# RWKV6 attention and a gated dense layer in one kernel: the boot in written order, level 16 copied by ScalarE, and h - tanh(h) of the first block summed by an accumulating transfer

## The chip, the cores and the metric

One core of a Trainium2 chip. TensorE multiplies matrices; VectorE and ScalarE work element by element; SyncE and GpSimd here mostly issue transfers, which the 16 DMA engines carry out. The metric is the device time of an execution in microseconds (us), taken as the median of several. Executions of one kernel here lie within about 1% of each other; all the runs told below are in the fast state, so they may be compared. The runs came in batches, a1 to a4 on another chip than b1, a5 to a7 and a10 to a13, so between batches the ratio to the kernel before is the safer measure. Profiles are of single executions of the same kernels; a profiled span is some 2 us shorter than the time of the same execution.

## The reference

```python
# attention: B, H, S, D = 4, 8, 768, 48; state is (B, H, D, D), starts at 0
for t in range(S):
    y[:, :, t] = einsum('bhd,bhde->bhe', r_t, state + (u * k_t) v_t^T)
    state = w_t[..., None] * state + k_t v_t^T
x = y.transpose(0, 2, 1, 3).reshape(3072, 384)
# dense part: w_in 384 x 2048, w_out 2048 x 384, both float64 in memory
h = x @ w_in
g = h - tanh(h)
out = g @ w_out
```

The recurrence is computed in chunks of 64 tokens, doubling a block size m: for m = 1, 2, 4, 8, 16 and 32 TensorE forms the products of one half of each block with the other ("level m"), VectorE multiplies by decays between levels, then come "turn" (transposes), "update" (states) and "result". In the program kq, rp, wt and v hold k, r, w and v of a block; kmix and rmix are k and r with every second token multiplied by u, for level 1. xT is the result as the dense part reads it; its last part lands in `late`, from which six small transfers fill the holes of xT.

## The kernel before

The 3072 tokens go through in 8 blocks of 384. The dense part of a block has 16 steps f of 128 columns of w_in. A step is three matmuls into `hp`, six ScalarE instructions, five VectorE instructions, and three steps later three matmuls into `acc`. The attention of block i+1 is woven into the steps of block i as phases. Block 0 has nobody ahead of it: its attention is the boot, and during boot and block 0 the float64 weights are converted as well, two ScalarE and three VectorE instructions for each f.

```python
def convert(f, raw, _):
    ...
    nc.scalar.activation(out=a.bitcast(F32), in_=hi.bitcast(F32), func=AF.Copy, scale=HIGH_SCALE)
    nc.scalar.activation(out=up, in_=lo.bitcast(U32), func=AF.Copy, scale=2.0 ** -29)
    return [
        lambda: nc.vector.tensor_single_scalar(a, a, 3, op=ALU.logical_shift_left),
        lambda: nc.vector.scalar_tensor_tensor(out=a, in0=hi, scalar=-2 ** 31, in1=a,
                                               op0=ALU.bitwise_and, op1=ALU.bitwise_or),
        lambda: nc.vector.tensor_tensor(out=a, in0=a, in1=up, op=ALU.add)]

def first(xT, f, ps):
    hp = ps.tile([P, NB], F32, name="hp", tag="hp")
    for kc in range(KC):
        nc.tensor.matmul(hp, lhsT=w_in_sb[:, f, kc, :], rhs=xT[:, kc, :], ...)
    ...
    nc.scalar.activation(out=h, in_=hp, func=AF.Copy, scale=1.0 / UPSCALE)
    nc.scalar.activation(out=s, in_=h, func=AF.Square)
    nc.scalar.activation(out=qa, in_=s, func=AF.Square, bias=shift[:, 0:1])
    nc.scalar.activation(out=qb, in_=s, func=AF.Square, bias=shift[:, 1:2])
    nc.scalar.activation(out=th, in_=h, func=AF.Tanh)
    nc.scalar.activation(out=big, in_=s, func=AF.Relu, bias=shift[:, 2:3])
    ...
    return g, [
        product(hs, h, SERIES, s, ALU.mult),
        lambda: nc.vector.tensor_tensor(out=th, in0=h, in1=th, op=ALU.subtract),
        product(hs, qa, QUAD[0][1], hs, ALU.add),      # a series for small h
        product(g, qb, QUAD[1][1], hs, ALU.add),
        lambda: nc.vector.copy_predicated(out=g, mask=big.bitcast(I32), data=th)]

# plan of block 0: at which f each phase of block 1 stands, and where weights are converted
names = ("level 1", 2, 4, 8, 16, 32, "turn", "update", "result")
steps = (1, 2, 3, 4, 5, 6, 8, 10, 12)
before = {0: ("kmix", "rmix", "totals 1", "totals 2", "kq")}   # kmix, rmix: times u, on VectorE
converted = (0, 3, 4, 5, 5, 8, 9, 10, 11, 11)

ctx.enter_context(tc.manual_schedule(engines={PE, SP}))   # boot: VectorE, ScalarE ordered by the scheduler
```

The VectorE instructions of step f are issued behind the ScalarE instructions of step f+1, with the conversions between them.

Of the kernel before, what the change touches and what calls it, by code (L numbers as in the profile page):

```python
# [83 lines left out]
def kernel(  # L84
# [24 lines left out]
    for i, value in enumerate((QUAD[0][0], QUAD[1][0], -SMALL)):  # L109
# [9 lines left out]
    mask_cols = {1: slice(0, 64), 2: slice(64, 96), 4: slice(96, 128), 8: slice(128, 160),  # L119
                 16: slice(160, 192)}  # L120
    mask_all = const.tile([P, 192], I8, name="mask_all", tag="mask_all")
# [60 lines left out]
    class Block:  # L182
# [27 lines left out]
        def mix(self, p0, n):  # L210
            rmix, kmix, rp, kq = (self.tiles[x] for x in ("rmix", "kmix", "rp", "kq"))

            def part(t, p, k, odd):
                return t[:, p * NB:(p + k) * NB].rearrange("d (n two) -> d n two", two=2)[:, :, odd]

            for t, src, odd in ((kmix, kq, 1), (rmix, rp, 0)):
                nc.vector.tensor_copy(out=part(t, p0, n, 1 - odd), in_=part(src, p0, n, 1 - odd))
                for p in range(p0, p0 + n):
                    nc.scalar.activation(out=part(t, p, 1, odd), in_=part(src, p, 1, odd),  # L219
                                         func=AF.Copy, scale=u_sb[:, p:p + 1])  # L220
# [21 lines left out]
        def level_1(self, ps, p0):  # L242
            gr = self.gram(ps, self.tiles["kmix"], self.tiles["rmix"], p0, UP, 1, L)
            mask = masks[1].bitcast(U8).rearrange("s b j -> s (b j)").unsqueeze(1).unsqueeze(1)
            nc.vector.copy_predicated(
                out=A[:, :, p0:p0 + UP].rearrange("s h p c t -> s h (p c) t"),
                mask=mask.to_broadcast([P, 2, UP * NCP, L]),
                data=gr.rearrange("s h (n t) -> s h n t", t=L))
# [24 lines left out]
        def level(self, ps, m, p0, n):  # L273
            if m == L // 2:
                self.last_level(ps, p0, n)
                return self.decay(m, p0, n)
            gr = self.gram(ps, self.tiles["kq"], self.tiles["rp"], p0, n, m, L // 2)
            ins = self.decay(m, p0, n)
            nb = L // (2 * m)
            for h in range(2):  # L280
                dst = A[:, h, p0:p0 + n].rearrange("s p c (b two m) -> s (p c) b two m",
                                                   two=2, m=m)[:, :, :, 1, :]
                src = gr[:, h].rearrange("s (n b m) -> s n b m", b=nb, m=m)
                mask = masks[m].bitcast(U8).unsqueeze(1).to_broadcast([P, n * NCP, nb, m])
                nc.vector.copy_predicated(out=dst, mask=mask, data=src)  # L285
            return ins
# [39 lines left out]
        def update(self, ps, p0):  # L326
# [17 lines left out]
            for c in range(NCH - 1 if last else NCH):  # L344
                for p in range(UP):
                    dst = St[:, p0 + p, c + 1, 0:D] if c + 1 < NCH else                         states[self.q + 1][:, p0 + p, 0, 0:D]
                    n0 = (p * NCP + c // 2) * D
                    k = (i0 + p) * NCH + c
                    nc.vector.scalar_tensor_tensor(  # L349
                        out=dst, in0=St[:, p0 + p, c, 0:D], scalar=tot[:, k:k + 1],  # L350
                        in1=kvp[:, c % 2, n0:n0 + D], op0=ALU.mult, op1=ALU.add)

# [57 lines left out]
        def phase(self, ps, name):  # L410
            if name == "level 1":
                for p0 in HALVES:
                    self.level_1(ps, p0)
# [36 lines left out]
        def start(self, ps, background):  # L450


            for p0 in HALVES:
                for name, src in (("kq", kT), ("rp", rT), ("wt", wT)):
                    self.load(name, src, p0, UP)
            for name in ("rmix", "kmix"):
                self.tiles[name] = inp.tile([P, NPAIR * NB], F32, name=name, tag=name)
            yield
            for p0 in HALVES:
                self.mix(p0, UP)  # L460
                self.level_1(ps, p0)
                self.decay(1, p0, UP)
                self.totals(1, p0, UP)
            for m in (2, 4, 8, 16, 32):
                for p0 in HALVES:
                    ins = self.level(ps, m, p0, UP)
                    self.totals(m, p0, UP)

                tc.add_manual_dep(background.pop(0)().ins, ins.ins.name, mybir.DependencyInfo(
                    mybir.DependencyClass.Sync, mybir.DependencyReason.DATA))  # L470
            for p0 in HALVES:
                self.turn(ps, p0)
            background.pop(0)()
            for p0 in HALVES:
                self.update(ps, p0)
            for p0 in HALVES:
                self.result(ps, list(range(p0, p0 + UP)), p0 != HALVES[0])
                if p0 == HALVES[0]:
                    self.fill_holes([nc.sync, nc.scalar, nc.sync, nc.scalar, nc.sync, nc.sync])
            yield  # L480


    def first(xT, f, ps):
# [13 lines left out]
        nc.scalar.activation(out=th, in_=h, func=AF.Tanh)  # L497
# [4 lines left out]
        def product(out, in0, scalar, in1, op0):  # L502
# [4 lines left out]
            product(hs, h, SERIES, s, ALU.mult),  # L507
            lambda: nc.vector.tensor_tensor(out=th, in0=h, in1=th, op=ALU.subtract),  # L508
# [24 lines left out]
    def plan(i):  # L533

        names = ("level 1", 2, 4, 8, 16, 32, "turn", "update", "result")
        if i == 0:

            steps = (1, 2, 3, 4, 5, 6, 8, 10, 12)
            before = {0: ("kmix", "rmix", "totals 1", "totals 2", "kq")}
            behind = {1: ["rp"]}  # L540
            converted = (0, 3, 4, 5, 5, 8, 9, 10, 11, 11)
# [9 lines left out]
    ctx.enter_context(tc.manual_schedule(engines={PE, SP}))  # L551
    with tc.tile_pool(name="ps_boot", bufs=4, space=PSUM) as boot:
        xT = blocks[0].begin()
        raws = []

        def more_weights():
            raws.append(load_weights(len(raws), nc.sync))
            return raws[-1][-1]

        def ahead(name, src):  # L560
            return lambda: blocks[1].load(name, src, 0, NPAIR)

        background = [ahead("rmix", rT), ahead("kmix", kT), ahead("wt", wT)]
        background += [more_weights for _ in range(3, RAWS)] + [ahead("kq", kT)]
        start = blocks[0].start(boot, background)
        next(start)
        more_weights()
        blocks[0].load_v()
        for f in (1, 2):
            more_weights()  # L570
        next(start)
        for f in range(AHEAD):
            for op in convert(*raws.pop(0)):
                op()
            raws.append(load_weights(f + RAWS, nc.gpsimd))
    ps_d = ctx.enter_context(tc.tile_pool(name="ps_d", bufs=1, space=PSUM))
    ps_a = ctx.enter_context(tc.tile_pool(name="ps_a", bufs=2, space=PSUM))
    with tc.manual_schedule(engines={DVE, ACT}):
        blocks[1].prepare("load 3")
        waiting, rest, extra = [], [], []  # L580
        loaded = AHEAD + RAWS
        for i, blk in enumerate(blocks):
            here = xT
            later = blocks[i + 1] if i + 1 < len(blocks) else None
            after = blocks[i + 2] if i + 2 < len(blocks) else None
            if later:
                xT = later.begin()
            phases, before, behind, converted = plan(i)
            second = Second(blk.b * S + blk.q * NB, ps_d)
            for f in range(NF):  # L590
                g, next_rest = first(here, f, ps_d)
                waiting.append((second, f, g))

                for n, op in enumerate(rest):
                    op()
                    if n >= 2 and extra:
                        extra.pop(0)()
                for op in extra:
                    op()
                rest = next_rest  # L600
                if later:
                    for name in before.get(f, ()):
                        later.prepare(name)
                    if f in phases:
                        later.phase(ps_a, phases[f])
                    for name in behind.get(f, ()):
                        block = after if name.startswith("load") else later
                        if block:
                            block.prepare(name)
                extra = []  # L610
                for _ in range(converted.count(f)):
                    extra += convert(*raws.pop(0))
                    if loaded < NF:
                        raws.append(load_weights(loaded, nc.gpsimd))
                        loaded += 1
                if len(waiting) > LAG:
                    s, fs, gs = waiting.pop(0)
                    s.add(fs, gs)
        for op in rest:
            op()  # L620
        for s, fs, gs in waiting:
            s.add(fs, gs)
# [47 lines left out]
```

## Time and profile before

The time is 679.96 us in the runs at hand before the prediction. What matters of its profile, with the rows themselves in the prediction below:

| event | us |
|---|---|
| state updates of the boot begin | 33.55 |
| first dense matmul (hp) | 49.47 |
| level-2 products of block 1 begin | 63.58 |
| level-32 products of block 1 begin, after a wait of 1.55 | 88.93 |
| last acc matmul of block 0 ends | 146.6 |
| profiled span | 678.6 |

The prediction reads it in three stretches: the boot, block 0, and the rest, in which TensorE is busy 99% of the time. So the table is a list of milestones: a gain is one only if the last acc of block 0 comes earlier, and nothing behind it is made longer.

### The profile page before, as it was taken

The page shows a single profiled execution, that of the slowest core. Times are in us where ns is not written, and L with a number is a line of the kernel's source. Part 1 is how long each engine was busy: PE and PEld are TensorE (multiplying, and loading weights), DVE is VectorE, ACT ScalarE, POOL GpSimd, SP SyncE. Part 2 cuts the span into 40 slices and gives each one's busy share as a digit, 9 for nine tenths or more (in the row PEclk, how much of TensorE's full clock was granted, in tenths as well). Part 3 has the DMA queues.
Part 4 walks back from the last instruction along what each step waited for, and adds up shares of the span by engine and source line. Part 5 has one row for each costly group of instructions (what it writes and reads, how often), then busy time and mean ns, then how long its engine had stood idle before and what let it go on. Part 6 is the DMA issues. An engine that isn't in the chain of part 4 may idle for free.

```text
span 678.6 us, 19964 instructions
## 1 busy us (share of the span) xinstructions
PE 643.7 (95%) x8480; PEld 412.9 (61%) x8480; DVE 567.3 (84%) x1139; ACT 470.2 (69%) x920; POOL 9.8 (1%) x30
## 2 busy tenths in 40 slices
PE   3847999999999999999999999999999999999997
PEld 3734656656665666656665666656666566655554
DVE  7899999999986998689984999769986899756764
ACT  4346779985677757686576856777576865768785
POOL 2010000000000000000000000000000000000000
PEclk9968989999999999999999999999999999999999
DMA  8788141204012321025012140124110200001000
GB/s 312 219 286 319 67 140 47 92 36 142 2 50 90 98 80 50 10 82 176 3 48 92 36 141 3 48 90 142 38 48 15 98 17 2 1 11 36 0 0 36
DMA packets 30840, 54.36 MB, mean 80 GB/s; under 512 B 2336, under 2 KB 28704, under 8 KB 30752
## 3 DMA queue, kind: packets, MB, share of 16 engines
q1 hardware_dynamic: 28960, 44.20, 19.6%
q0 software_dynamic: 1584, 8.65, 3.6%
q8 instruction: 67, 1.10, 0.7%
q10 hardware_dynamic: 208, 0.25, 0.1%
q14 instruction: 21, 0.17, 0.1%
HBM read 47.19 MB, written 4.72 MB: 76 GB/s over the span
## 4 chain that ended last, share of the span: by engine, by line
PE 78%; DVE 7%; issue 4%; PEld 4%; DMA 3%; ACT 3%; PEldq 0%; SPq 0%; DVEq 0%; ACTq 0%
PE acc L524 33%; PE hp L486 31%; PE att L238 9%; DVE states L349 2%; PE att L386 2%; PEld hp L486 2%; PE att L321 2%; PEld att L368 1%; DMA raw<-in_weights 1%; PE att L302 1%; DMA xT<-late 1%; PEld acc L524 1%; DMA wt<-in_wT 1%; DVE kq L270 1%; DVE hs L503 1%
## 5 line engine op out<-in xcount | busy, mean ns | idle before, releaser
L486 PE MATMUL hp<-xT,w_sb 128*128 128x384 f32 x768 | 273.4, 493 | 8.4 <-DMA xT<-late 6.8
L524 PE MATMUL acc<-w_sb,gT 128*128 128x384 f32 x768 | 275.0, 495 | 0.0
L486 PEld LDWEIGHTS hp<-xT,w_sb 128*128 128x128 f32 x768 | 147.6, 193 | 112.5 <-ACT up L169 7.0
L524 PEld LDWEIGHTS acc<-w_sb,gT 128*128 128x128 f32 x768 | 140.7, 190 | 89.2 <-ACT o L529 2.3
L493 ACT ACTIVATE h<-hp 128x384 f32<-128x384 f32 x128 | 62.7, 490 | 163.0 <-PE hp L486 162.4
L508 DVE TENSOR_TENSOR th<-h,th 128x384 f32<-128x384 f32 x128 | 70.9, 554 | 43.2 <-ACT th L497 43.1
L503 DVE SCALAR_TENSOR_TENSOR hs<-h,s 128x384 f32<-128x384 f32 x128 | 71.0, 555 | 23.2 <-ACT s L494 23.0
L511 DVE COPY_PREDICATED gT<-big,th 128x384 f32<-128x384 int32 x128 | 76.1, 595 | 12.8 <-ACT th L497 0.5
L495 ACT ACTIVATE qa<-s,shift 128x384 f32<-128x384 f32 x128 | 78.8, 615 | 4.2
L503 DVE SCALAR_TENSOR_TENSOR gT<-qb,hs 128x384 f32<-128x384 f32 x128 | 71.4, 558 | 9.7 <-PE hp L486 0.5
L498 ACT ACTIVATE big<-s,shift 128x384 f32<-128x384 f32 x128 | 76.8, 600 | 0.0
L496 ACT ACTIVATE qb<-s,shift 128x384 f32<-128x384 f32 x128 | 76.7, 599 | 0.0
L503 DVE SCALAR_TENSOR_TENSOR hs<-qa,hs 128x384 f32<-128x384 f32 x128 | 70.6, 551 | 0.0
L494 ACT ACTIVATE s<-h 128x384 f32<-128x384 f32 x128 | 67.0, 524 | 4.1
L238 PEld LDWEIGHTS att<-rp,kq 48*64 48x64 f32 x3072 | 54.7, 148 | 22.5 <-issue 18.9
L497 ACT ACTIVATE th<-h 128x384 f32<-128x384 f32 x128 | 64.9, 507 | 0.0
L238 PE MATMUL att<-rp,kq 48*64 48x32 f32 x3072 | 58.4, 231 | 6.1 <-issue 6.0
L270 DVE TENSOR_TENSOR kq<-kq,tot 128x768 f32<-128x768 f32 (+1 forms) x45 | 38.7, 859 | 2.6 <-PE att L238 2.6
L285 DVE COPY_PREDICATED scores<-mask_all,att 128x384 f32<-128x384 uint8 (+1 forms) x72 | 40.3, 621 | 0.0
L270 DVE TENSOR_TENSOR rp<-rp,tot 128x768 f32<-128x768 f32 (+1 forms) x45 | 38.8, 863 | 0.0
L349 DVE SCALAR_TENSOR_TENSOR states<-states,tot,att 128x48 f32<-128x48 f32 x176 | 31.5, 256 | 6.7 <-PE att L339 6.7
L238 PE MATMUL att<-rmix,kmix 48*64 48x64 f32 x768 | 14.5, 232 | 8.8 <-ACT rmix L219 6.1
(50 smaller groups left out, 338.8 us busy)
## 6 DMA issues: line engine op xcount, KB each, us to landing
raw<-in_weights POOLq DMA_DIRECT2D x11, 768.0 KB, 6.7
rmix<-in_rT SPq DMA_DIRECT2D x7, 768.0 KB, 4.7
kmix<-in_kT SPq DMA_DIRECT2D x7, 768.0 KB, 6.5
wt<-in_wT SPq DMA_DIRECT2D x7, 768.0 KB, 7.3
kq<-in_kT SPq DMA_DIRECT2D x7, 768.0 KB, 4.4
rp<-in_rT SPq DMA_DIRECT2D x7, 768.0 KB, 4.8
v_sb<-in_v SPq DMA_DIRECT2D x8, 576.0 KB, 5.7
out_y<-o SPq DMA_DIRECT2D x23, 192.0 KB, 2.0
```

What stands on the lines that cost most here:

```text
L238: nc.tensor.matmul(dst, lhsT=lhs[rows, t0:t0 + L], rhs=src, start=True, stop=True)
L270: ins = nc.vector.tensor_tensor(out=part, in0=part, in1=by, op=ALU.mult)
L486: nc.tensor.matmul(hp, lhsT=w_in_sb[:, f, kc, :], rhs=xT[:, kc, :], start=(kc == 0), stop=(kc == KC - 1))
L494: nc.scalar.activation(out=s, in_=h, func=AF.Square)
L495: nc.scalar.activation(out=qa, in_=s, func=AF.Square, bias=shift[:, 0:1])
L496: nc.scalar.activation(out=qb, in_=s, func=AF.Square, bias=shift[:, 1:2])
L497: nc.scalar.activation(out=th, in_=h, func=AF.Tanh)
L498: nc.scalar.activation(out=big, in_=s, func=AF.Relu, bias=shift[:, 2:3])
L503: return lambda: nc.vector.scalar_tensor_tensor(out=out, in0=in0, scalar=scalar, in1=in1, op0=op0, op1=ALU.mult)
L508: lambda: nc.vector.tensor_tensor(out=th, in0=h, in1=th, op=ALU.subtract),
L511: lambda: nc.vector.copy_predicated(out=g, mask=big.bitcast(I32), data=th)]
L524: nc.tensor.matmul(acc, lhsT=g[:, j * P:(j + 1) * P], rhs=w_out_sb[:, f, :], start=(f == 0), stop=(f == NF - 1))
```

## The change

The intent is to relieve VectorE where it is the fuller engine, and to start the dense part earlier. Five things are done at once: the boot is written out in order for VectorE and ScalarE, with two whole conversions ahead of the state updates; block 1's two multiplications by u go to ScalarE in the boot; level 16 needs no mask any more and is copied by ScalarE; in block 0 tanh(-h) is computed and a transfer of GpSimd adds h to it, in place of VectorE's subtraction; phases, conversions and weight loads are put at other places. Core of the diff:

```diff
-    ctx.enter_context(tc.manual_schedule(engines={PE, SP}))
+    ctx.enter_context(tc.manual_schedule(engines={PE, SP, DVE, ACT}))
@@ level: no mask for level 16
+            if 2 * m % 32 == 0:
+                for par in range(2):
+                    for b in range(nb):
+                        ...
+                        nc.scalar.copy(out=dst[:, :, :, t0:t0 + m], in_=src[:, :, :, b, :])
+                return ins
@@ first
-        nc.scalar.activation(out=th, in_=h, func=AF.Tanh)
+        nc.scalar.activation(out=th, in_=h, func=AF.Tanh, scale=-1.0 if by_dma else 1.0)
+        if by_dma:
+            nc.gpsimd.dma_start(out=th, in_=h, accum_op=ALU.add)
...
-            product(hs, h, SERIES, s, ALU.mult),
-            lambda: nc.vector.tensor_tensor(out=th, in0=h, in1=th, op=ALU.subtract),
+            product(hs, h, SERIES, s, ALU.mult)] + ([] if by_dma else [
+            lambda: nc.vector.tensor_tensor(out=th, in0=h, in1=th, op=ALU.subtract)]) + [
@@ plan of block 0
-            steps = (1, 2, 3, 4, 5, 6, 8, 10, 12)
-            before = {0: ("kmix", "rmix", "totals 1", "totals 2", "kq")}
+            steps = (1, 2, 3, 5, 7, 9, 10, 11, 13)
+            before = {0: ("totals 1", "totals 2", "kq")}
-            converted = (0, 3, 4, 5, 5, 8, 9, 10, 11, 11)
+            converted = (0, 3, 3, 4, 5, 6, 10, 10, 11, 12)
@@ boot (written out; cut to its end)
+            if m <= 8:
+                ready.append(convert(*raws.pop(0)))
+            if m in (8, 16):
+                later.mix(0, NPAIR, ("rmix" if m == 8 else "kmix",), copies=False)
+        converted()
+        for p0 in HALVES:
+            blk.turn(ps, p0)
+        converted()
+        for _ in range(2):
+            ready.append(convert(*raws.pop(0)))
+        begin_behind(blk.update(ps, h1), later.load("kq", kT, 0, NPAIR))
+        begin_behind(blk.update(ps, h2), more_weights(nc.sync))
+        blk.result(ps, [h1, h1 + 1])
+        blk.fill_holes([nc.sync, nc.scalar, nc.sync, nc.scalar, nc.sync, nc.sync])
+        blk.result(ps, [h2, h2 + 1], True)
+        converted()
+        more_weights(nc.sync)
+        later.load("rp", rT, 0, NPAIR)
+        more_weights(nc.sync)
+        later.load_v()
+        ...
@@ main loop
-            g, next_rest = first(here, f, ps_d)
+            g, next_rest = first(here, f, ps_d, i == 0)
```

## The prediction

> **What bounds the kernel now.** I read first the table of busy time in three stretches: up to the first matmul of the dense part (49.5 us), block 0 of the dense part (to 127 us), and the rest. Columns: PE, PEld, DVE, ACT, POOL busy us (instructions), granted clock, DMA share, GB/s.
>
> ```profile
> 0.00:49.50 49.50, 26.96 (x877) 24.53 (x877) 41.32 (x106) 22.00 (x38) 6.66 (x24) 0.90 0.81 268
> 49.50:127.00 77.50, 71.66 (x1010) 45.14 (x1011) 75.84 (x141) 61.00 (x111) 3.17 (x6) 0.91 0.39 133
> 127.00:675.00 548.00, 545.09 (x6596) 343.25 (x6594) 450.19 (x894) 386.75 (x771) 0.00 (x0) 1.00 0.17 55
> ```
>
> From 127 us on TensorE is busy 545.1 of 548 us at full clock: nothing that spares VectorE or ScalarE shortens that part. Everything to win lies ahead of it: 49.5 us of boot, in which the dense matmuls can't start, and block 0, where VectorE is busy 75.8 of 77.5 us and TensorE waits and runs below full clock.
>
> Second, the timeline of boot and block 0 (start, length, instruction, idle before it):
>
> ```profile
> 33.55 4.29 DVE L349 SCALAR_TENSOR_TENSOR states<-states,tot,att 128x48 f32<-128x48 f32 x24 [0.60 <-PE att L339]
> 41.25 0.92 ACT L168 ACTIVATE w_sb<-raw 128x768 f32<-128x768 f32 x1 [2.32 <-DMA raw<-in_weights]
> 42.06 0.47 ACT L399 COPY late<-att 128x384 f32<-128x384 f32 x1
> 42.56 2.49 SPq L406 DMA_DIRECT2D xT<-late  x4
> 49.47 4.04 PE L486 MATMUL hp<-xT,w_sb 128*128 128x384 f32 x6 [6.84 <-DMA xT<-late]
> 58.79 2.20 PE L486 MATMUL hp<-xT,w_sb 128*128 128x384 f32 x6 [0.89 <-ACT h L493]
> 62.53 0.94 DVE L270 TENSOR_TENSOR rp<-rp,wt 128x768 f32<-128x768 f32 x1
> 63.58 2.79 PE L238 MATMUL att<-rp,kq 48*64 48x32 f32 x96 [2.58 <-issue]
> 66.30 4.17 PE L486 MATMUL hp<-xT,w_sb 128*128 128x384 f32 x6
> 88.93 1.01 PE L302 MATMUL att<-rp,kq 48*32 48x32 f32 x96 [1.55 <-DVE rp L270]
> 144.69 2.10 PE L524 MATMUL acc<-w_sb,gT 128*128 128x384 f32 x6
> ```
>
> The boot ends thus: ScalarE stands behind a weight load that lands at 41.2 us, so the copy to "late" comes at 42.06 though the matmuls behind it were done near 38.7; the six small transfers that fill the holes of xT then need 6.7 us; the first dense matmul starts at 49.47. In block 0 the level-2 products start only at 63.58: the profile says "issue", but the decay of rp that they read ends at 63.47, so I read it as a wait for VectorE. After that wait three hp matmuls (x6, each counted twice) take 4.17 us, against 2.1 at full clock. The last acc of block 0 (f=15) starts at 144.69 and ends at 146.6; I measure the change by that end, as all after it is TensorE-bound.
>
> Third, the groups whose durations I use and the two sizes of transfer that matter:
>
> ```profile
> L508 DVE TENSOR_TENSOR th<-h,th 128x384 f32<-128x384 f32 x128 | 70.9, 554 | 43.2 <-ACT th L497 43.1
> L311 ACT COPY scores<-att 32x192 f32<-32x192 f32 x8 | 2.5, 310 | 7.9 <-PE att L302 7.8
> raw<-in_weights POOLq DMA_DIRECT2D x11, 768.0 KB, 6.7
> out_y<-o SPq DMA_DIRECT2D x23, 192.0 KB, 2.0
> ```
>
> The subtraction costs 0.554 us each, but neighbours on VectorE start 0.47 us apart at this size and 0.87 us at 128x768; I use the spacings.
>
> **What the Trainium skill says.** "TensorE: Matmul & The Clock Gate", What's actually happening: TensorE runs at half rate after an idle window of about 3.4 us and needs a busy one of that length to recover. The trace agrees in kind: clock 0.50 from 65 to 70 us after the stalls of 58 to 63.5, 1.00 from 75 on; a pause of 2.6 us was enough here, so waits count nearly double. "DMA: Bandwidth & Descriptors", SWDGE vs HWDGE vs iDMA: accumulation during a transfer is possible only from GpSimd; Anatomy of one DMA gives 2.0 us plus bytes/436 GB/s for such a transfer, so by that page 192 KB is an estimated 2.5 us. The trace has a plain 192 KB from SyncE at 2.0 us in quiet time, but 24 KB took 6.7 us among weight loads; no accumulating transfer is in this trace. "SBUF — State Buffer", Who interferes with whom: VectorE's two-port modes block GpSimd's descriptor writing. Here GpSimd's issues took 0.53 us each, most of them beside a busy VectorE, so I take it as small.
>
> **The change part by part.**
>
> Boot, VectorE. The order of its instructions is the same to level 16, but for four small copies less (level 16: 0.31 us each, 1.25 in all). The second half still waits for TensorE's products, so of the 1.25 I count 0.65: level 32 ends at 30.5 instead of 31.1. Then the written order puts two whole conversions (6 instructions, 2 x 2.2 us) ahead of the state updates; before, there were three instructions. States start at about 34.9 instead of 33.55: 1.3 us lost, end 39.2.
>
> Boot, ScalarE. It gets 8 level-16 copies (8 x 0.31 = 2.5 us, like L311) and 8 multiplications by u (0.41 each, 3.3 us), between 20.4 and 28.1, where it was idle for 7.8 us. They delay the level-32 copies and the turn by some 2 us, just hidden behind the two conversions. In return the copy to "late" no longer stands behind a weight load: products at about 39, late and xT done at 40 instead of 42.5. Ahead of the six transfers there are then one kq load (from 37) and one weight load (from 39), 1.5 MB, which at the 300 GB/s of 36 to 48 us is 5 us from 39.5: landing near 45. The second half of xT: products at 43, four copies (1.9 us, as before) to 45. First dense matmul 45 to 46 instead of 49.5.
>
> Block 0 up to level 2: VectorE's chain from the end of the states. After: conversions f=2 to 5, 4 x 2.2 = 8.8 to 48.0; totals 2.6 (52.1 to 54.7 before) to 50.6; kq decay 0.9 to 51.5; rest of f=0 with conversion f=6, three of 0.47, 2.2, copy 0.5 = 4.1 to 55.6; two mask copies 1.8 to 57.4; rp decay 0.9 to 58.3. Before, this point was 63.5: the two multiplications by u are gone (1.8), one subtraction (0.5), and gaps. So 5 us are won here, and the start of the dense matmuls at 45 is not what sets it: TensorE again pauses, now about 4 us ahead of level 2, and again runs that product and three hp at half clock.
>
> Block 0 from level 2 on. VectorE is relieved of 14 more subtractions (6.6 us) and the two level-16 copies (0.9), and the phases are spread to later f. Step by step VectorE: level 4 done at 69.3 (before 75.2), level 8 at 83, level-16 decays at 93, level 32 at 98.6, states 110.5, f=12 at 119 (before about 130). TensorE from 58.4: level 2 in 2.8, hp f=3 in 4.2, then each f 3.87 us (hp and acc at 1.94) plus its products (1.6; level 32 1.0; turn 1.35; result 3.3): level 16 at 84, level 32 at 93.6 against decays ready at 93, the turn within 0.2 us of its decays, acc f=15 ends at about 138.5. TensorE is thus just bound by itself from 58.4 on. 146.6 - 138.5 = 8 us won.
>
> Weights are now loaded from SyncE's queue; at the rate at which they are used, one per 4 to 7 us, a load is there in time.
>
> Later blocks: level 16 costs ScalarE four copies (0.47 each, about 1.9 us a block) and spares VectorE 0.9; ScalarE is at 71% and TensorE never waits for it: zero.
>
> Sum: 680 - 8 = 672.
>
> **The rivals.**
>
> First, the accumulating transfer becomes the wait. ScalarE's th of f=0 ends near 50, its consumer on VectorE stands at 54.5, a slack of 4.5 us; for f=1 it is 5.7; from f=2 on 6 to 10; at f=14 and 15 some 2 to 3, where TensorE is three f behind. For: in this stretch rp, v, weights and block 2's loads are under way, the same sort of load in which 24 KB took 6.7 us. Against: 2.0 us for 192 KB when quiet. If each takes 7 to 8 us, f=0 and f=1 delay level 2 by 2 to 3 us: 674 to 675. I have let this push the centre from 671.7 to 672. At 12 us and more VectorE would stand in each f: 680 or above.
>
> Second, with VectorE relieved, TensorE never pauses long enough to lose its clock. Its own work from 45 to the end of acc f=15 is 82 us at full clock (16 f of 3.87 plus about 14 of products, plus three hp of the next block): 127, so 660 us. Against: VectorE's chain to level 2 is conversions, which the change does not shorten.
>
> Third, ScalarE becomes the bound: in block 0 about 16 x 3.05 + 10 x 1.65 + 7.6 = 73 us of the 82. hp has one buffer, so a late h stops TensorE directly. Where two conversions (3.3 us) stand in one f, h of the next comes later than TensorE asks for it by at most 1 us. Worth 1 to 3 us.
>
> Fourth, the loads on SyncE stand in order, one that waits for its buffer holding up those behind; a late kq or weight would cost some us. Loads are needed 5 us and more after issue, so I give it little.
>
> **Range and chances.** The rivals on the slow side give 674 to 677, the optimistic side 667 and with luck 660; the range is 667 to 677.5. Faster by over 2% means below 666.4, more than double clock luck: 0.09. Slower would need transfers of over 15 us: 0.01.
>
> **What would show it.** In the changed kernel: first hp matmul at 45 to 46; xT filled in about 5 us; states ending near 39; level-2 products at 58 to 59 with the clock at half after them; level 32 waiting less than a microsecond; no subtraction on VectorE before block 1; th transfers of 3 to 6 us with VectorE hardly idle before its copy to gT; end of block 0's last acc near 138.5; busy time of TensorE after it unchanged. It is wrong if VectorE's idle time is put down to the transfer into th for more than 3 us, if hp starts after 47, or if the stretch behind block 0 changes its length.

## The result, and the profile after

The changed kernel takes **686.5 us** (median of 4, 685.27 to 687.55) against 679.27 us before. The ratio is 1.0106, with a 95% interval of 1.008 to 1.0133: within 2%, but slower, and well above the predicted range of 667 to 677.5. A ratio here and below is worked out from the runs of both kernels in the same batch, so it is not quite the ratio of the medians that are quoted.

The same three stretches of the changed kernel, in the table of busy time (PE, PEld, DVE, ACT, POOL busy us with instructions, granted clock, DMA share, GB/s):

```profile
0.00:49.50 49.50, 31.29 (x881) 27.91 (x882) 41.19 (x102) 27.25 (x54) 5.04 (x19) 1.00 0.74 253
49.50:127.00 77.50, 65.79 (x990) 41.90 (x988) 67.42 (x122) 61.77 (x112) 11.17 (x13) 0.91 0.60 176
127.00:675.00 548.00, 542.50 (x6597) 342.20 (x6598) 443.03 (x877) 397.26 (x796) 2.93 (x3) 1.00 0.18 56
```

VectorE was relieved as planned, from 75.8 to 67.4 us in the middle stretch. But TensorE, which sets the end, is busy there for 65.8 us instead of 71.7. It had been busy for 4.3 us more in the first stretch (31.29 against 26.96), because the dense part starts earlier; to 127 us that leaves 97.1 against 98.6, and in the last stretch it is 542.5 instead of 545.1. The relieved engine didn't pull the other one along. The timeline of the changed kernel (start, length, instruction, idle before it and what ended it) says where TensorE stood:

```profile
35.95 4.28 DVE L360 SCALAR_TENSOR_TENSOR states<-states,tot,att 128x48 f32<-128x48 f32 x24
46.69 4.05 PE L466 MATMUL hp<-xT,w_sb 128*128 128x384 f32 x6 [2.94 <-DMA xT<-late]
53.75 0.89 POOL L480 DMA_DIRECT2D th<-h  x1 [5.80 <-ACT th L478]
62.64 0.59 DVE L494 COPY_PREDICATED gT<-big,th 128x384 f32<-128x384 int32 x1 [5.76 <-DMA th<-h]
66.81 2.78 PE L240 MATMUL att<-rp,kq 48*64 48x32 f32 x96 [8.60 <-issue]
142.25 0.60 DVE L494 COPY_PREDICATED gT<-big,th 128x384 f32<-128x384 int32 x1 [5.84 <-DMA th<-h]
147.82 2.10 PE L507 MATMUL acc<-w_sb,gT 128*128 128x384 f32 x6
163.17 1.60 PE L240 MATMUL att<-rp,kq 48*64 48x32 f32 x96 [1.82 <-DVE scores L247]
```

The dense part does start earlier, at 46.69 instead of 49.47. Then the first transfer is issued at 53.75 us, and VectorE stands 5.76 us in front of the copy that needs it. Behind that copy stand the masked copies of level 1 and the decay of rp, without which level 2 can't start: TensorE pauses for 8.6 us, and level 2 begins at 66.81, 3.2 us later than before. The last acc of block 0 (the row at 147.82 ends at 149.75, where the next hp begins) is 3.1 us later than before. A second wait of 5.84 us comes at 142.25, for the transfer of f=14. Its consequence is in the last row: block 1's level 2 waits 1.82 us for VectorE, at a place where TensorE of the kernel before waits for nothing. Together these are 4.9 us; the profiled span grew by 4.6 (678.6 to 683.2). The profiled execution was the fastest of the four.

One row of the groups gives the sum of VectorE's idle time before those copies and what ended most of it:

```profile
L494 DVE COPY_PREDICATED gT<-big,th 128x384 f32<-128x384 int32 x128 | 76.2, 595 | 24.5 <-DMA th<-h 11.9
```

Of the 16 transfers only three were waited for, 11.9 us in all, and two of them make 11.6. So it is not that the transfer is slow as such. Among the transfers under way between 46 and 62 us are these (size, us from issue to landing):

```profile
raw<-in_weights SPq DMA_DIRECT2D x2, 768.0 KB, 12.9
rp<-in_rT SPq DMA_DIRECT2D x1, 768.0 KB, 10.6
...
kmix<-in_kT SPq DMA_DIRECT2D x1, 768.0 KB, 13.5
v_sb<-in_v SPq DMA_DIRECT2D x1, 576.0 KB, 13.7
th<-h POOLq DMA_DIRECT2D x3, 192.0 KB, 6.7
```

Loads of these kinds land within 4.7 to 6.4 us in the median of the whole kernel and need 10.6 to 13.7 us here: the DMA engines are busy nearly throughout, at 358 GB/s in the mean, and the 192 KB share them. The first transfer took 8.8 us, the next two 6.7 and 6.4; quiet ones took 2.9 (f=3, 8, 9, 11). At f=14 rp and v of block 2 had been issued at 134.43 and 135.04, just ahead of the transfer at 135.44, which took 6.7.

### The profile page after: what moved, and what is told of

Read it like the earlier page. It is cut to its first block, busy times and chain, and to the rows that moved or that the text cites. A ratio compares the mean times of both kernels' runs of the same rounds, so it can differ in the third digit from the quotient of the medians.

```text
span 683.2 us, 20039 instructions
## 1 busy us (share of the span) xinstructions
PE 644.4 (94%) x8480; PEld 414.5 (61%) x8480; DVE 553.6 (81%) x1103; ACT 488.0 (71%) x964; POOL 19.1 (3%) x35
## 4 chain that ended last, share of the span: by engine, by line
PE 70%; issue 10%; DVE 6%; PEld 4%; DMA 4%; ACT 3%; POOL 1%; PEldq 1%; SPq 0%; DVEq 0%; POOLq 0%; ACTq 0%
PE acc L507 30%; PE hp L466 28%; PE att L240 8%; DVE states L360 2%; DMA th<-h 2%; PE att L398 2%; PEld att L380 2%; PEld hp L466 2%; PE att L332 1%; PEld acc L507 1%; DMA xT<-late 1%; PE att L313 1%; DMA wt<-in_wT 1%; POOL th L480 1%; DVE hs L486 1%
## 5 line engine op out<-in xcount | busy, mean ns | idle before, releaser
L491 DVE TENSOR_TENSOR th<-h,th 128x384 f32<-128x384 f32 x112 | 62.2, 555 | 43.3 <-ACT th L478 43.3
L494 DVE COPY_PREDICATED gT<-big,th 128x384 f32<-128x384 int32 x128 | 76.2, 595 | 24.5 <-DMA th<-h 11.9
L296 DVE COPY_PREDICATED scores<-mask_all,att 128x384 f32<-128x384 uint8 (+1 forms) x54 | 31.9, 657 | 0.0
L240 PE MATMUL att<-rmix,kmix 48*64 48x64 f32 x768 | 14.5, 232 | 9.3 <-ACT rmix L220 6.3
```

The costliest lines, as they stand in the source:

```text
L240: nc.tensor.matmul(dst, lhsT=lhs[rows, t0:t0 + L], rhs=src, start=True, stop=True)
```

## The experiments

All runs gave correct results, one of them although it was wrong on purpose (a5_plain). The medians of the kernel before in the batches were 680.13 us (a1 to a4), 679.91 (b1, a5, a7, a6), 679.75 (a10 to a12) and 679.59 (a13). The theory: two transfers collide with loads, and the rest of the change is worth little because VectorE still sets the time up to level 32. The rivals: the boot, the level-16 copies, or the accumulation itself is the loss.

### The whole change without the transfer (a1_none)

```diff
-            g, next_rest = first(here, f, ps_d, i == 0)
+            g, next_rest = first(here, f, ps_d, False)
```

> The changed kernel with the subtraction h - tanh(h) back on VectorE for every f, all else kept. Theory (two waits): the changed kernel loses because VectorE twice stands about 5.8 us for an accumulating transfer that landed late (f=0: 8.8 us, f=14: 6.7 us) among loads of inputs and weights; the rest of the change wins some 2 to 3 us. Then: level-2 products of block 1 start near 61.5 us instead of 66.8, and the time is 677 to 681. Rival 1 (the new boot and the new phases are themselves no gain or a loss): 684 or more. Rival 2 (VectorE's relief matters more than the waits): VectorE-bound again, above 682.

Measured: 678.61 us, ratio 0.9969 (0.9944 to 0.9993). So the transfers cost 7.9 us (686.5 - 678.6), and the rest of the change wins 1.5 us (680.13 - 678.61), not 8. The changed kernel was timed in an earlier batch; by the ratios the transfers cost 1.37%, or 9.3 us, so differences against its 686.5 are uncertain by 1 us or more. Timeline of TensorE in this run:

```profile
60.89 2.79 PE L240 MATMUL att<-rp,kq 48*64 48x32 f32 x96 [2.87 <-issue]
97.90 1.01 PE L313 MATMUL att<-rp,kq 48*32 48x32 f32 x96 [1.83 <-DVE rp L272]
104.07 1.53 PE L332 MATMUL att<-ident,kq 128*128 128x128 f32 x12 [1.09 <-DVE kq L272]
122.66 0.42 PE L398 MATMUL att<-scores,v_sb 64*48 64x64 f32 x11 [0.57 <-issue]
```

Level 2 stands at 60.89 without any transfer: 2.7 us earlier than before, where 5.2 were predicted. From there to the end of the last acc (144.4) are 83.5 us; the kernel before has 83.0 (63.58 to 146.6) and the changed one 82.9 (66.81 to 149.75). That stretch was predicted at 80.1, TensorE's own work, and TensorE is indeed busy for only 79.9 of the 83.5. Of the rest, 2.9 us are waits for VectorE, at level 32 and at the turn, as the rows show; 0.57 us is a wait in the middle of the result products (last row) for nothing that the profile shows. VectorE has no time over (window from 50 to 150 us, columns as above):

```profile
50.00:150.00 100.00, 91.98 (x1083) 57.47 (x1082) 96.15 (x182) 83.94 (x157) 0.00 (x0) 0.97 0.37 132
```

### Transfers for f=3 to 13 only (a2_f3to13)

```diff
-            g, next_rest = first(here, f, ps_d, i == 0)
+            g, next_rest = first(here, f, ps_d, i == 0 and 3 <= f <= 13)
```

> The changed kernel with the accumulating transfer for f=3 to 13 of block 0 only; f=0,1,2,14,15 on VectorE. Theory (two waits): both waits gone, level 2 near 61.5 us, block 0's last acc ends near 144.5; time 676 to 679, at or below the run with no transfer at all by 0 to 3 us, as VectorE keeps the relief where the transfers land in 3 to 6.6 us. Rival (transfers disturb VectorE or the loads anywhere): as slow as 683 and more.

Measured: 678.42 us, ratio 0.9966 (0.9942 to 0.999). Eleven transfers are now nearly free: VectorE's waits have them at 1.5 us in two, as their row shows (us in total, times, longest). They aren't all quick, f=4 took 7.1 us and f=7 6.3; but VectorE comes for them late enough:

```profile
DVE gT L494 <- DMA th<-h: 1.5, 2, 0.9
```
The window from 50 to 150 us has VectorE 3.9 us less busy than in a1_none:

```profile
50.00:150.00 100.00, 92.82 (x1083) 57.19 (x1082) 92.30 (x170) 83.95 (x157) 9.56 (x11) 0.96 0.50 150
```

And yet the time is that of a1_none. Eleven subtractions off VectorE bring nothing that can be measured: level 32 comes at 97.41 instead of 97.90 and still waits 1.68 us. Only four of the eleven stand ahead of level 32. By VectorE's timelines each of these shortens its step by 0.18 to 0.28 us, and one wait of 0.61 us (f=4) goes against it. The turn is then 0.97 us ahead (103.10 against 104.07), but TensorE's wait in the result products is longer here, and the last acc ends at 144.7, no earlier than the 144.4 of a1_none:

```profile
122.97 0.42 PE L398 MATMUL att<-scores,v_sb 64*48 64x64 f32 x11 [1.50 <-issue]
```

This wait stands in all the kernels with the new boot (0.57 to 1.74 us) and not in the kernel before at this place; what ends it isn't shown. So it may hide a relief of up to a microsecond.

### The early and the late transfers by themselves (a3_f3to15, a4_f0to13)

```diff
# a3_f3to15
+            g, next_rest = first(here, f, ps_d, i == 0 and f >= 3)
# a4_f0to13
+            g, next_rest = first(here, f, ps_d, i == 0 and f <= 13)
```

> Accumulating transfer for f=3 to 15: takes away the first wait only. Theory: level 2 near 61.5, the wait of about 5.8 us at f=14 stays and costs block 1 some 2 us: 679 to 682. If the late wait costs nothing: equal to the run with f=3 to 13.

> Accumulating transfer for f=0 to 13: takes away the late wait only. Theory: the first wait of 5.8 us stays and level 2 stays at 66.8; only the wait of TensorE in block 1 (1.8 us before level 2 there) goes: 684 to 685.5. If the late wait is the main one: below 682.

Measured: a3_f3to15 683.22 us, ratio 1.0032 (0.9999 to 1.0064); a4_f0to13 682.75 us (680.4 to 686.06), ratio 1.0019 (0.9987 to 1.0051). Against a2_f3to13 the two late transfers cost 4.8 us and the three early ones 4.3; the sum of 9.1 stands against 8.1 for all five (686.5 - 678.4). Both were a little off what I had expected, the late ones on the slow side and the early ones on the fast side. In the timeline of a3_f3to15 one sees how a late wait costs so much:

```profile
137.15 0.60 DVE L494 COPY_PREDICATED gT<-big,th 128x384 f32<-128x384 int32 x1 [6.25 <-DMA th<-h]
158.08 2.63 PE L240 MATMUL att<-rp,kq 48*64 48x32 f32 x96 [2.35 <-DVE scores L247]
```

VectorE makes up only a part of the 6.25 us; 20 us later TensorE waits 2.35 us for it, and then runs the level-2 products at half its clock: 2.63 us, against 1.60 in the run of the result. Beside a2_f3to13 the trace tells the two apart: level 2 of block 1 begins 1.8 us later (158.08 against 156.24), and level 4, behind the stretch at half clock, 5.1 us later (166.93 against 161.84). The profiled spans differ by 4.6 (675.7 and 680.3). So here more is lost to the clock than to the wait. In the changed kernel the clock stays full after the late wait, with 5.60 us from level 2 to level 4. That may be why the profiled execution of the changed kernel, whose mean clock of 0.989 was above the 0.982 to 0.985 of the other three, was the fastest; no run settles that. The early wait is there in a4_f0to13 as in the changed kernel, 5.79 us ahead of the copy at 63.25.

### The transfer alone in the kernel before (b1_dma)

```diff
# in the kernel before: the same edit of first() as in the change, nothing else
-                g, next_rest = first(here, f, ps_d)
+                g, next_rest = first(here, f, ps_d, i == 0)
```

> The kernel before with one part of the change alone: in block 0 the subtraction is done by the accumulating transfer for every f (old boot, old phases, old level 16). Theory (the transfer shares the DMA engines with loads and VectorE waits for it): waits of 3 to 6 us at f=0 and again near f=13 to 15; time 681 to 686, slower than before although VectorE loses 16 subtractions. Rival (the transfer is a gain with the old boot, because VectorE is the bound): 677 or less.

Measured: 682.3 us, ratio 1.0021 (0.9975 to 1.0068). VectorE waits four times, 1.25 to 2.25 us (3 to 6 were expected). The first wait, 1.62 us, and a first hp that comes 0.5 us later put level 2 at 65.93 instead of 63.58. VectorE's busy time from 50 to 150 us falls from 96.46 to 88.36, without gain:

```profile
50.00:150.00 100.00, 91.40 (x1076) 57.13 (x1076) 88.36 (x158) 78.46 (x145) 17.23 (x22) 0.94 0.54 150
```

The waits are shorter than in the changed kernel (other loads lie beside these transfers, presumably for that reason), and the interval includes equality; but the transfer brings nothing without the new boot either.

### A plain transfer instead of an accumulating one (a5_plain)

Wrong on purpose: `th` becomes h. The comparison with the reference passed all the same.

```diff
-            nc.gpsimd.dma_start(out=th, in_=h, accum_op=ALU.add)
+            nc.gpsimd.dma_start(out=th, in_=h)
```

> The changed kernel with a plain transfer from GpSimd in place of the accumulating one (th is overwritten with h: a wrong result on purpose; where h is large the output differs). Same bytes, queue, order and waits. Theory (latency comes from the loads that share the engines): f=0 still lands after 7 to 9 us, f=14 after 5 to 7, the two waits stay above 4 us each, time within 2 us of the changed kernel. Rival (the addition in the transfer is what is slow): in quiet stretches 2.0 us instead of 2.9, waits under 2 us, time 680 or less.

Measured: 680.83 us, ratio 1.0006 (0.9957 to 1.0056), so 5.7 us faster than the accumulating kernel: the expectation, that only the collision counts, missed. From issue to landing, the view of the tile th gives for the changed kernel:

```profile
DMA to landing us min/median/max: 2.9/4.5/8.8
```
and with plain transfers:

```profile
DMA to landing us min/median/max: 2.1/3.0/6.1
```

By these two profiles the accumulation costs 0.8 us in quiet and 2.7 and 1.6 us among loads (f=0: 8.8 to 6.1; f=14: 6.7 to 5.1). The first wait falls to 3.22 us, the late one to 3.91:

```profile
60.31 0.59 DVE L494 COPY_PREDICATED gT<-big,th 128x384 f32<-128x384 int32 x1 [3.22 <-DMA th<-h]
```

A plain transfer would thus still have waited. Of the first wait, 2.5 us are due to the accumulation and 3.2 to the rest. But the time is only 2.2 us above a1_none (680.83 - 678.61), against 7.9 with accumulation: after a late wait of 3.91 us block 1's level 2 waits 0.19 us, after one of 5.84 it waited 1.82. So the larger part of the loss comes with the accumulation. The queue of GpSimd on the two pages (packets, MB, share of the time of 16 engines), first the changed kernel, then a5_plain:

```profile
q0 software_dynamic: 2592, 4.72, 3.3%
q0 software_dynamic: 1312, 4.72, 1.7%
```

Bytes are the same, packets are not: in a quiet stretch (f=8) an accumulating transfer is 144 packets and a plain one 64. GpSimd's issue also takes longer, 0.86 us against 0.54. The Trainium skill, "DMA: Bandwidth & Descriptors", Rules for kernel authors, says that an accumulate reads its destination and writes it later. A further stream of bytes doesn't show in these counts; whether the packets are the whole reason isn't shown.

### The loads moved away from the first transfers (a7_quiet)

```diff
# v of block 1 behind f=6, block 2's first loads behind f=5, one weight load less at f=0
-            behind = {1: ["rp"]}
+            behind = {1: ["rp"], 6: ["v"]}
-        for f, name in ((steps[0] + 1, "load 1"), ...
+        for f, name in ((5 if i == 0 else steps[0] + 1, "load 1"), ...
-        later.load_v()
-                if more_weights.n < NF:
+                if more_weights.n < NF and (i, f) != (0, 0):
```

> The changed kernel, transfer for every f, but with the loads that run beside f=0 moved away: v of block 1 loaded at f=6 instead of at the end of the boot, the loads of block 2 (rmix, kmix, wt) at f=5 instead of 2, one weight load at f=0 left out and made up later. Theory: f=0 lands in 3 to 5 us instead of 8.8, VectorE's wait there falls from 5.8 to under 2, level 2 starts at 63 or earlier; the late wait at f=14 stays: 679 to 683. Rival (latency has another cause): no change, 685 and more.

Measured: 690.79 us, ratio 1.0144 (1.01 to 1.0189), the slowest of all. The first transfer landed in 6.5 us instead of 8.8, its wait fell from 5.76 to 3.63 and level 2 came at 64.84, as a collision theory wants. But the moved loads then met the transfers of f=4 to 7, which took 9.0, 7.1, 6.5 and 6.7 us, and VectorE stood 3.59 us at 90 us and 5.52 late. As a remedy it failed: the bytes have to be moved in block 0 in any case, and the collision went with them.

### Level 16 back on VectorE (a6_l16dve)

```diff
-            if 2 * m % 32 == 0:
+            if False:      # and the mask for 16 is there again
```

> The changed kernel with level 16 copied by VectorE under its mask again, as before; all else kept. Theory: level 16 on ScalarE is worth next to nothing: within 2 us of the changed kernel's 686.5. Rival (the ScalarE copies delay the boot or the later blocks): 684 or less; rival (they are a real gain): 689 or more.

Measured: 687.55 us, ratio 1.009 (1.0046 to 1.0134), against 686.5 and 1.0106 for the changed kernel. The two can't be told apart: moving level 16 is worth nothing that shows, in block 0 or later.

### Work taken off the chain to level 2 (a10_defer, a11_defer_none, a12_defer_states)

If TensorE were bound by itself from level 2 on, an earlier level 2 would be an earlier end. These kernels convert three weights fewer ahead of level 2 and spread them over later f. a10_defer has the transfers of f=3 to 13, a11_defer_none has none, and a12_defer_states is a10_defer with the ScalarE multiplication of kmix behind the turn in the boot and the second conversion behind the state updates.

```diff
-            converted = (0, 3, 3, 4, 5, 6, 10, 10, 11, 12)
+            converted = (1, 2, 3, 3, 4, 5, 6, 8, 10, 10, 11, 12)
-        for _ in range(2):
-            ready.append(convert(*raws.pop(0)))
+        ready.append(convert(*raws.pop(0)))
...
-        ready.append(convert(*raws.pop(0)))
# a12_defer_states, on top of it
-            if m in (8, 16):
-                later.mix(0, NPAIR, ("rmix" if m == 8 else "kmix",), copies=False)
+            if m == 8:
+                later.mix(0, NPAIR, ("rmix",), copies=False)
-        converted()
+        later.mix(0, NPAIR, ("kmix",), copies=False)
```

> The kernel with the transfer for f=3 to 13 only, and three of the weight conversions that VectorE does ahead of level 2 (f=4, 5, 6; 2.6 us each) moved behind it. Question: is TensorE bound by itself from level 2 on, as the prediction said, or by VectorE as far as level 32? First: level 2 starts about 4 us earlier (near 57, then hp of f=2 sets it) and the time falls by the same 4 us, to 674 to 675. Second (VectorE is busy without a gap up to level 32, so that what is put off is only done later): level 2 starts earlier, TensorE's waits at level 16, 32 and the turn grow, time 676.5 to 679, at most 2 us won.

> The same deferral with no accumulating transfer at all (subtraction on VectorE for every f). If VectorE's relief by the 11 transfers has any worth, it shows here, where level 2 no longer waits for the conversions: slower than the run with transfers by 1 to 3 us. If they are within 1 us of each other, the transfer is worth nothing even where it is never waited for.

> As the deferral with the transfer for f=3 to 13, and ScalarE multiplies kmix by u behind the copies of the turn instead of ahead of level 32, so that the state updates start earlier. Expected: ScalarE's copies of the turn at about 31.6 instead of 33.2, states near 34.5 to 35.5 instead of 35.95 (the two conversions on VectorE then set it), first hp about 1 us earlier, level 2 about 1 us earlier; the time 0 to 1.5 us below the deferral alone. If the boot's end does not set anything, the same time.

Measured over 5 rounds: 681.09 us, ratio 0.9997 (0.9956 to 1.0037); 682.12, ratio 1.0013 (0.998 to 1.0045); 679.89, ratio 0.999 (0.9955 to 1.0025). None beats a2_f3to13 by its ratio (0.9966), though the intervals overlap, and the 681.09 of a10_defer lies above both forecasts. TensorE's timeline in a10_defer:

```profile
65.49 2.78 PE L240 MATMUL att<-rp,kq 48*64 48x32 f32 x96 [2.60 <-DVE rp L272]
98.77 1.01 PE L313 MATMUL att<-rp,kq 48*32 48x32 f32 x96 [1.63 <-DVE rp L272]
106.27 2.76 PE L332 MATMUL att<-ident,kq 128*128 128x128 f32 x12 [2.42 <-DVE kq L272]
```

Level 2 did come at 59.16 (58.69 in a11_defer_none), earlier than in the kernels above, but level 4 then waits (65.49), and level 32 comes at 98.77, later than the 97.41 of a2_f3to13, although level 2 was 1.9 us ahead. It is 99.15 and 99.64 in the other two. An earlier start doesn't help, because up to level 32 VectorE's sum of work sets the time: in a10_defer it is busy for 38.4 of the 39 us from 60 to 99. What is put off is only waited for later. In a12_defer_states the state updates begin at 35.42 instead of 35.90, about as forecast, but the first hp comes at 46.31 (46.39) and level 2 at 59.32 (59.16): the states don't set them. Between a11_defer_none and a10_defer the 1 us is within the noise.

### GpSimd subtracts by an instruction (a13_gpsimd)

```diff
-        nc.scalar.activation(out=th, in_=h, func=AF.Tanh, scale=-1.0 if by_dma else 1.0)
+        nc.scalar.activation(out=th, in_=h, func=AF.Tanh)
-            nc.gpsimd.dma_start(out=th, in_=h, accum_op=ALU.add)
+            nc.gpsimd.tensor_tensor(out=th, in0=h, in1=th, op=ALU.subtract)
```

> The changed kernel, but GpSimd subtracts tanh(h) itself, by an instruction, for all 16 f of block 0; no transfer of th at all. Theory (what hurts is only the transfer's latency among the loads): nothing in it depends on the DMA engines, so VectorE's waits at f=0 and f=14 fall below 1 us if GpSimd needs 1 to 2 us for 128x384; level 2 near 61; 677 to 679, like the runs without transfer. Rival (GpSimd and VectorE disturb each other at SBUF): VectorE's instructions beside it get longer, and it is slower than the run with no transfer: 681 or more.

Measured over 5 rounds: 682.72 us, ratio 1.0031 (0.9994 to 1.0069). GpSimd needs 1.0 to 1.7 us (once 3.07) for a subtraction, and VectorE no longer stands for a transfer; level 2 comes at 62.97, of which 1.4 us against a1_none is a first hp that began later (47.85 against 46.45). But VectorE's instructions beside it grow longer. One such instruction of this run in the timeline:

```profile
55.03 1.37 DVE L486 SCALAR_TENSOR_TENSOR hs<-h,s 128x384 f32<-128x384 f32 x1
```
The group of its kind from 50 to 140 us (count, busy us, mean ns):

```profile
L486 DVE SCALAR_TENSOR_TENSOR hs<-h,s 128x384 f32<-128x384 f32 x15 | 10.7, 713 | 0.0
```
The same group in a1_none:

```profile
L486 DVE SCALAR_TENSOR_TENSOR hs<-h,s 128x384 f32<-128x384 f32 x17 | 9.4, 551 | 0.0
```

1.37 us instead of 0.55, and 713 ns in the mean instead of 551. This is what the Trainium skill, "SBUF — State Buffer", Who interferes with whom, says of a VectorE instruction with two inputs in SBUF beside a GpSimd instruction that reads SBUF; the trace agrees and gives the size. The rival of the expectation came true. The subtraction gained nothing in any other place: on GpSimd it lengthened VectorE's own instructions, and as a transfer that nobody waits for it was worth nothing that shows (a2_f3to13).

## Why the prediction was wrong

It said 672 us, 667 to 677.5, and the time was 686.5. The class, within 2%, was the likeliest one, but the direction was wrong. The difference of 14.5 us goes by its own milestones:

| step | predicted | without transfers (a1_none) | changed kernel | share of the miss, us |
|---|---|---|---|---|
| level 2 begins | 58.4 | 60.89 | 66.81 | 2.5 + 5.9 |
| from there to the end of the last acc of block 0 | 80.1 | 83.5 | 82.9 | 2.8 |
| from there to the end of the run, at the profiled time | 533.5 | | 535.5 | 2.0 |
| profiled execution to the median | | | 685.27 to 686.5 | 1.2 |

(The 533.5 are 672 - 138.5; the 535.5 are 685.27 - 149.75.)

**First step that failed: "the accumulating transfer becomes the wait", first rival.** The mechanism was right, and even the places were named, f=0 and f=14. The size was not. It put the slack of f=0 at 4.5 us, took "7 to 8 us" as the bad case and made 2 to 3 us of it. The slack was 3.4 us (th ends at 53.45, VectorE is there at 56.88), the transfer took 8.8, and the wait was 5.76. It weighed the bad case lightly because 192 KB had needed 2.0 us in quiet, when the same trace showed that 24 KB had needed 5.9 to 6.5 us among such loads (medians of the two queues; the 6.7 of the prediction are all six together). It had no row for what an accumulation costs: 0.8 us more than a plain one in quiet, 1.6 and 2.7 us more in the crowd (a5_plain).

**Second: "at f=14 and 15 some 2 to 3, where TensorE is three f behind".** The slack of TensorE was taken for a slack of VectorE. VectorE did stand for 5.84 us, and a part of what it owed came due in block 1: 4.8 us in the time by a3_f3to15 against a2_f3to13. It also hit the statement that all after block 0 is TensorE-bound and keeps its length. That held in a1_none (531.4 us to the end of the span, 532.0 before) and not here (533.4).

**Third: "VectorE's chain from the end of the states".** The mark was 58.4; without transfers it was 60.89. A conversion was taken at 2.2 us, and took 2.56 in the boot (39.69 to 42.25 in a1_none). The spacing of 0.47 us holds between neighbours that don't depend on each other. The timeline of the changed kernel shows both kinds:

```profile
53.86 0.55 DVE L486 SCALAR_TENSOR_TENSOR hs<-h,s 128x384 f32<-128x384 f32 x1
54.52 0.56 DVE L486 SCALAR_TENSOR_TENSOR hs<-qa,hs 128x384 f32<-128x384 f32 x1
54.99 0.56 DVE L170 TENSOR_SCALAR w_sb<-w_sb 128x768 int32<-128x768 int32 x1
```

The second reads what the first writes and starts 0.66 us after it; the third is independent of the second and starts 0.47 us after it. So a subtraction that stood between two dependent instructions was partly free: taking it out saves an estimated 0.66 - 2 x 0.47 = -0.28, that is 0.28 us and not 0.47, where no conversion stands there in its place; a2_f3to13 measured 0.18 to 0.28. The states ended at 40.2 instead of 39.2, and the first dense matmul came at 46.7 instead of 45 to 46. (The "300 GB/s of 36 to 48 us" in that sum is a misreading: the trace of the kernel before has 271 there.)

**Fourth: "TensorE is thus just bound by itself from 58.4 on".** It was counted to 80.1 us of its own work, and TensorE was busy for 79.9 in a1_none: the sum was right. But VectorE stood at 96 of 100 us beside it, and TensorE's waits for it at level 32 (1.83) and the turn (1.09), with the unexplained 0.57 in the result products, made it 83.5. In a1_none, in a2_f3to13 with 3.9 us less on VectorE, in the kernel before and in the changed one the stretch has the same length within 0.7 us (a2_f3to13: 61.06 to 144.7). The counted 6.6 us of relief by 14 subtractions are worth nothing that shows.

**What was right.** Level 16 on ScalarE is zero (a6_l16dve). Level 2 and three hp after the pause run at half clock (2.78 us for the products at 66.81, against 1.60 at full clock). GpSimd's issue is small, 0.85 to 0.89 us and once 1.22. The copy to "late" no longer stands behind a weight load, and the dense part starts earlier. That a wait for the transfer into th of more than 3 us would mean a wrong prediction was said, and is what happened.

**The best version.** a1_none (678.61 us) and a2_f3to13 (678.42 us) are some 0.3% faster than the kernel before, with intervals that just exclude equality. a1_none is the simpler one: the change without its transfer.

**What stays open.** Why more than twice the packets cost more among loads than in quiet; what TensorE waits for in the result products of block 1; and why the clock fell after some pauses of TensorE and not after others of the same length.

## What to carry to other kernels

A transfer that takes an instruction's place has to be measured beside the loads that will run with it, not by its quiet time: here 192 KB took 2.9 us in quiet and 8.8 us in the crowd, and two waits of nearly 6 us ate all that the change won. A relieved engine shortens nothing while its relief doesn't reach the wait that ends last, and a late wait of an engine that has little time over is paid for at the next place that needs that engine, here 20 us later. When a change of many parts goes wrong, first run it without its boldest part; that one run split the miss here into 7.9 us for the transfers and the rest.

## What the Trainium skill lacked or had wrong

- "DMA: Bandwidth & Descriptors" gives no cost for an accumulating transfer. From its fit, 192 KB is an estimated 2.5 us; here a plain one of GpSimd took 2.1 us in quiet (so the fit is near), an accumulating one 2.9, and among loads that filled the DMA engines 6.1 and 8.8. No page says that an accumulating transfer goes in more packets: here 144 against 64 for the same bytes.
- The same page's fit says nothing of a transfer that shares the DMA engines with loads: those of 768 KB from SyncE took 10.6 to 13.5 us when issued from 46 to 62 us, against medians of 4.7 to 6.4 over the kernel.
- "SBUF — State Buffer" names the contention of VectorE's two-input instructions with a GpSimd instruction that reads SBUF, but no size for this pair: here 0.55 us became 1.37 in one case, and 551 ns became 713 in the mean.
- "VectorE: DVE Perf Modes", The DRAIN you can't avoid, says of a row of eight copies that a semaphore after each costs nothing extra, and gives no cost for one instruction that waits for another. Here, at 128x384, an instruction that reads what its neighbour wrote starts 0.58 to 0.67 us after it, an independent one 0.47 us.
- "TensorE: Matmul & The Clock Gate" puts the idle window at about 3.4 us; here a pause of 2.35 us ahead of block 1's level 2 (a3_f3to15) was followed by products at half clock (2.63 us against 1.60). The length of the pause alone didn't decide it: after 1.87 us at the same place in a7_quiet the clock fell to 0.50 (168 to 170 us), after 2.42 us in a6_l16dve it stayed full.
